# Where ScalarE empties a finished pair's bank in a slot of attention, which slots take the low parts of rows on GpSimd, and three casts of weights that change their slot

## The chip, the cores and the metric

The kernel runs on one core of a Trainium2 chip. The metric is the device time of one execution in microseconds (us). Before the change it is 763.03 us, the median of three runs (762.01 to 764.55).

## The reference, cut to what matters

For 2048 tokens of 512 features, all in fp32:

```
xn  = layernorm(x)
qkv = xn @ wqkv                       # 32 heads of 16 features each
p   = softmax(mask(q k^T / 4))        # a query sees itself and the 255 keys before it
s   = (p v) @ wo
h   = gelu(layernorm(xn) @ w1 + b1)   # 512 -> 1792
g   = silu(h @ w2 + b2)               # 1792 -> 512
out = x + s * g
```

## The kernel before, in words

**Number format.** A matrix product is made of three products of fp32r parts: a value is split into a high part (a cast) and a low part (the value less its high part), and high x high, high x low and low x high are added up. So every operand needs a cast, mostly on ScalarE, and a subtraction, on VectorE or GpSimd.

**Slots.** The attention is a hand-written schedule of 128 slots, `for t in range(-16, end + 1)` near the end of `mixer_kernel`: slot t handles group n = t // 16 of four heads and key block t % 16 of 128 keys. Every recorded instruction stands at L42, the line of the helper that keeps program order, so groups are told apart by their tiles' names. One slot issues, in this order on TensorE:

1. `prob_block(n, kb, 1)`: two matmuls of scores into the tile `stb`, which is one pair of banks for all slots; ScalarE's exponential reads it and writes `pt`; GpSimd then cuts `pt` at the band's edges (two selects).
2. `max_block` for 12 slots ahead: scores into `xy` and, where there is a block two back, into columns 0 to 255 of `zo`; VectorE merges them with a predicated copy and reduces them to row maxima (`mt`).
3. `fill_in(t, 0)`: a share of other work (below), then the entries of `plan` for slot t, which `at` puts there: casts, low parts, DMA issues.
4. `prob_block(n, kb, 0)`: the second two matmuls into `stb`, the second exponential, two more selects.
5. `fill_in(t, 1)`: more of the other work.
6. `pv_step`: 24 matmuls of the slot before into `otb`, columns 256 to 383 of the second bank of `zo`, which ScalarE copies out to `oraw`.
7. the entries of `ends`, which `behind` puts there: mostly DMA issues.

Every engine does its instructions in that order. The next slot's step 1 writes `stb` again, so it waits until the second exponential has read it.

**Tandems.** The other work of slots 3 to 127 is `tandem(t0, t1, one, two)`: two products of 512 columns made at the same time, one on rows 0 to 63 and one on rows 64 to 127 of TensorE, in the banks `fb[0]` and `fb[1]`; a unit is one matmul of each. At the end slot t1 the pair is finished: `one` is copied out of `fb[0]` by ScalarE and `two` out of `fb[1]` by VectorE (the last two lines of `tandem`). The next tandem starts in slot t1 + 1 and its first unit writes `fb[1]` and then `fb[0]`. There are 22 tandems, with end slots 8, 14, 19, 24, 30, 35, 41, 47, 53 (projections of q and k: `pair_qk`), 58, 63, 68, 74 (of v: `pair_v`), 79, 84, 90, 98 (of q and k), and 104, 110, 115, 121, 127 (hidden units of the MLP: `pair_h`). Slots 91 and 92 hold transposes of y in `fb`, and slot 128 a product of the MLP in `fb[0]`.

**What a finished pair of q and k sets off.** `pair_qk.finish(ps, t, copy)` copies the bank to `pjr`, casts it to `sh` on ScalarE in slot `free` (t + 1 for the even chunk of 512 tokens, t + 3 for the odd one, or later if the rows are still in use; for the very first pair's even chunk in the end slot itself, through `behind`), sends the high rows by four DMAs of SyncE, subtracts on GpSimd in the slot that `quiet` gives (`pjr<-pjr,sh`), and sends the low rows by two DMAs. `quiet(t)` returns the first slot from t on that is 1 or 2 modulo 4 and not yet taken. Slots that are 3 modulo 4 end with GpSimd's work on the row maxima (`max_rows`).

**Weights.** `split_wqk` casts the q and k weights of the next group on ScalarE (`wqb<-wqkr`) and subtracts on VectorE; `fetch_wqk` loads them four slots ahead. `settle` does the same for slices of w1 (tile `xnT`) and w2 (tile `w`).

**After the slots** follow the MLP's products, the output projection and the gate, in which nothing is touched.

Of the kernel before, what the change touches and what calls it, by code (L numbers as in the profile page):

```python
# [49 lines left out]
def mixer_kernel(ctx, tc, x, wqk, wv, wo, w1, b1, w2, b2, out):  # L50


    nc = SimpleNamespace(**{name: Ordered(tc, name) for name in ("tensor", "vector", "scalar", "gpsimd", "sync")})
# [141 lines left out]
    fb = [psf.tile([P, 512], F32, name=f"fb{i}") for i in range(2)]  # L195
# [92 lines left out]
    fills = {}  # L288
# [71 lines left out]
    def pair_qk(n, c):  # L360
# [11 lines left out]
        def finish(ps, t, copy):  # L372
            hi = sgp.tile([P, 512], F32R, tag="sh", name=f"sh_{n}_{c}", bufs=2)
            raw = t2.tile([P, 512], F32, tag="t2", name=f"pjr_{n}_{c}")
            lo = raw.bitcast(F32R)
            copy(raw, ps)

            def send_high():
                if n >= 2:
                    copy_rows(slots[n % 2][3:P:32, 0, :, sl], slots[n % 2][7:P:32, 0, :, sl])  # L380
                for qk, tt in ((1, 0), (0, 0), (1, 2), (0, 1)):
                    send(hi, qk, tt)

            def send_low():
                send(lo, 1, 1)
                send(lo, 0, 2)


            free = t if (n, c) == (1, 2) else max(t + 1 + 2 * (c % 2), 16 * n - 28 + 4 * c)
            free += 2 * (t == 90)  # L390
            (behind if free == t else at)(free, nc.scalar.copy, hi, raw)
            behind(free, send_high)
            free = quiet(max(free, t + 1))
            at(free, lambda: nc.gpsimd.tensor_tensor(lo, raw, hi.bitcast(F32), op=ALU.subtract))
            behind(free, send_low)
        return 3 * KT, mm, finish

    def quiet(t):

        while t % 4 not in (1, 2) or t in taken:  # L400
            t += 1
        taken.add(t)
        return t

    taken = set()
# [28 lines left out]
    def tandem(t0, t1, one, two, mid=None, back=None):  # L434

        n = one[0]
        lo, hi = slice(0, 64), slice(64, P)
        mid = mid or max(1, (t0 + t1 + 1) // 2)  # L440
        most = n // 4

        def places(slots, last):

            last = min(most, n // (len(slots) + 1)) if last else 0
            cuts = [(n - last) * k // len(slots) for k in range(len(slots) + 1)]
            out = []
            for t, a, b in zip(slots, cuts, cuts[1:]):
                ahead = min(b - a, max(most, (b - a + 1) // 2))
                out += [(t, 0)] * ahead + [(t, 1)] * (b - a - ahead)  # L450
            return out + [(t1, 0)] * last

        first, second = places(range(t0, mid), False), places(range(back or mid, t1), True)
        for phase, where in enumerate((first, second)):
            for i in range(n):
                flags = dict(start=(phase == 0 and i == 0), stop=(phase == 1 and i == n - 1), skip_group_check=True)
                def unit(i=i, phase=phase, flags=flags):
                    (two if phase == 0 else one)[1](fb[1 - phase], i, hi, **flags)
                    (one if phase == 0 else two)[1](fb[phase], i, lo, **flags)
                fills.setdefault(where[i], []).append((unit, ()))  # L460
        fills[t1, 0].append((one[2], (fb[0], t1, nc.scalar.copy)))
        fills[t1, 0].append((two[2], (fb[1], t1, nc.vector.tensor_copy)))

    def spread(jobs, places):
# [180 lines left out]
    def at(t, fn, *args):  # L645
        plan.setdefault(t, []).append((fn, args))
# [36 lines left out]
    n, raw = raws["qk"]  # L683
# [25 lines left out]
    for place, todo in spread([job_qk(1, 0), job_qk(1, 1)], [(-2, 0), (-1, 1), (-1, 1), (-1, 1), (0, 0), (0, 1)] +  # L709
                              [(t, k) for t in (1, 2) for k in range(2)]).items():  # L710
        fills.setdefault(place, []).extend(todo)
    soon = {}
    tandem(3, 8, pair_qk(1, 2), pair_qk(1, 3))
    for n, spans in enumerate((((9, 14), (15, 19)), ((20, 24), (25, 30)), ((31, 35), (36, 41)), ((42, 47), (48, 53, 51)),
                               ((75, 79), (80, 84)), ((85, 90), (93, 98))), 2):
        for c, span in zip((0, 2), spans):
            tandem(*span[:2], pair_qk(n, c), pair_qk(n, c + 1), *span[2:])
    for i, (t0, t1) in enumerate(((54, 58), (59, 63), (64, 68), (69, 74))):
        tandem(t0, t1, pair_v(2 * i), pair_v(2 * i + 1))
    for f, *span in ((6, 99, 104, 102), (8, 105, 110), (10, 111, 115), (12, 116, 121, 118, 119), (2, 122, 127, 124, 125)):  # L720
        tandem(*span[:2], pair_h(f), pair_h(f + 1), *span[2:])

    for n, t in enumerate((-5, 5, 17, 28, 38, 70, 80), 1):
        at(t - 4, fetch_wqk, n)
        at(t, split_wqk, 0)
        at(t, split_wqk, 1)
    at(20, fetch_wv, 1)
    at(23, split_wv_part, 0)
    at(26, split_wv_part, 1)
# [8 lines left out]
    on_pool = nc.gpsimd  # L738
# [4 lines left out]
                 (1, 105), (4, 105), (5, 107)):  # L743
        at(t, fetch, "w1", f)
    for f, t, lo_at, lo_by in ((6, 94, 96, nc.vector), (7, 95, 97, on_pool), (8, 96, 98, on_pool), (9, 97, 100, nc.vector),
                               (10, 100, 101, nc.vector), (11, 101, 102, nc.vector), (12, 103, 105, on_pool),
                               (13, 105, 106, on_pool), (2, 106, 108, nc.vector), (3, 107, 109, on_pool),
                               (0, 108, 110, on_pool), (1, 109, 112, nc.vector), (4, 111, 113, on_pool),
                               (5, 112, 114, on_pool)):
        at(t, settle, "w1", f, nc.scalar.copy)  # L750
        at(lo_at, settle, "w1", f, None, lo_by)
# [92 lines left out]
    for f in range(6, NF, 2):  # L844
        t = gp.tile([P, 2, 512], F32, tag="ohl", name=f"hr_{f}", bufs=4)
# [421 lines left out]
```

## Time and profile before

| what | us |
|---|---|
| median of three runs | 763.03 (762.01 to 764.55) |
| the profiled execution, its own time | 761.15 |
| span of its instructions | 759.4 |
| TensorE matmuls busy | 742.0 |
| VectorE busy | 513.2 |
| ScalarE busy | 439.9 |
| GpSimd busy | 299.7 |

The profiled execution is 1.88 us under the median, and 1.75 us of its time lie outside the span. Times in timelines are us from the span's start: slot 0 starts at 63.8, slot 41 at 184.6 and slot 127 at 431.9. In a row of a timeline stand the start, the duration, the engine (PE is TensorE's matmuls, PEld its weight loads, DVE VectorE, ACT ScalarE, POOL GpSimd, SPq SyncE's queue), the operation, output <- inputs, the sizes, the number of instructions merged into the row, and in brackets how long the engine had been idle and what ended that. A usual slot takes 2.8 us. PE's matmul ends are modelled, and consecutive matmuls overlap in the rows.

### The profile page before, as it was taken

The page shows a single profiled execution, that of the slowest core. Times are in us where ns is not written, and L with a number is a line of the kernel's source. Part 1 is how long each engine was busy: PE and PEld are TensorE (multiplying, and loading weights), DVE is VectorE, ACT ScalarE, POOL GpSimd, SP SyncE. Part 2 cuts the span into 40 slices and gives each one's busy share as a digit, 9 for nine tenths or more (in the row PEclk, how much of TensorE's full clock was granted, in tenths as well). Part 3 has the DMA queues.
Part 4 walks back from the last instruction along what each step waited for, and adds up shares of the span by engine and source line. Part 5 has one row for each costly group of instructions (what it writes and reads, how often), then busy time and mean ns, then how long its engine had stood idle before and what let it go on. Part 6 is the DMA issues. An engine that isn't in the chain of part 4 may idle for free.

```text
span 759.4 us, 18803 instructions
## 1 busy us (share of the span) xinstructions
PE 742.0 (98%) x7428; PEld 580.8 (76%) x7428; DVE 513.2 (68%) x781; ACT 439.9 (58%) x746; POOL 299.7 (39%) x644
## 2 busy tenths in 40 slices
PE   9999999999999999999999999999999999999997
PEld 8886676666778887676676688888878888888886
DVE  7886776877776677887873548763667765676373
ACT  7747767867666676777777745444554643442001
POOL 6413757767566554767867700120102000001102
PEclk9999999999999999999999999999999999999999
DMA  8623355655457753546734383542113232254531
GB/s 287 185 63 82 87 131 135 169 116 121 99 124 234 244 177 90 140 113 169 191 100 158 97 296 102 177 146 74 41 30 109 84 112 70 69 162 130 170 93 56
DMA packets 56952, 99.40 MB, mean 131 GB/s; under 512 B 11104, under 2 KB 11360, under 8 KB 56864
## 3 DMA queue, kind: packets, MB, share of 16 engines
q1 hardware_dynamic: 56864, 98.21, 44.9%
q8 instruction: 58, 0.95, 0.5%
q14 instruction: 30, 0.25, 0.1%
HBM read 51.39 MB, written 29.62 MB: 107 GB/s over the span
## 4 chain that ended last, share of the span: by engine, by line
PE 88%; ACT 5%; DVE 2%; DMA 2%; issue 2%; POOL 1%; SPq 1%; ACTq 0%; DVEq 0%; POOLq 0%
PE acc L42 20%; PE fb L42 18%; PE zo L42 12%; PE p L42 9%; PE stb L42 8%; PE h L42 6%; PE s L42 6%; PE xy L42 5%; ACT pt L42 3%; PE pv L42 3%; POOL pt L42 1%; DMA x<-in_x_dram 1%; DMA qk<-pjr 1%; PE yt L42 1%; DVE xy L42 1%
## 5 line engine op out<-in xcount | busy, mean ns | idle before, releaser
L42 POOL TENSOR_SCALAR_AFFINE_SELECT pt<-pt 128x256 f32<-128x256 f32 x480 | 194.7, 430 | 138.2 <-ACT pt L42 135.0
L42 ACT ACTIVATE pt<-stb 128x768 f32<-128x768 f32 (+1 forms) x244 | 188.7, 773 | 54.8 <-PE stb L42 44.9
L42 DVE TENSOR_REDUCE mt<-xy 128x4 f32<-128x1024 f32 (+1 forms) x128 | 152.6, 1192 | 4.4
L42 PE MATMUL acc<-w,gh 128*128 128x512 f32 x432 | 134.6, 393 | 0.0
L42 DVE COPY_PREDICATED xy<-upper,zo 128x512 f32<-128x512 int32 x112 | 77.9, 696 | 76.5 <-PE zo L42 73.1
L42 PE MATMUL fb<-xnT,wqb 64*128 64x512 f32 (+1 forms) x684 | 114.7, 404 | 0.1
L42 POOL TENSOR_TENSOR xo<-xo,gated 128x512 f32<-128x512 f32 x15 | 20.2, 1350 | 219.0 <-DVE gated L42 195.2
L42 PE MATMUL stb<-qk 64*128 64x384 f32 (+1 forms) x488 | 97.6, 396 | 7.9 <-ACT pt L42 6.4
L42 PE MATMUL zo<-pt,vt 128*17 128x128 f32 x2880 | 103.8, 275 | 0.3
L42 PEld LDWEIGHTS zo<-pt,vt 128*17 128x17 f32 x2880 | 67.4, 97 | 36.7 <-issue 19.3
L42 PEld LDWEIGHTS acc<-w,gh 128*128 128x128 f32 x432 | 80.9, 188 | 17.2
L42 PEld LDWEIGHTS stb<-qk 64*128 64x128 f32 x488 | 45.6, 183 | 55.6 <-ACT pt L42 46.4
L42 PE MATMUL acc<-w,gl 128*128 128x512 f32 x216 | 84.4, 391 | 0.0
L42 PEld LDWEIGHTS fb<-xnT,wqb 64*128 64x128 f32 (+1 forms) x684 | 63.5, 186 | 6.9 <-issue 0.6
L42 PE MATMUL xy<-qk 64*128 64x256 f32 (+2 forms) x536 | 60.2, 298 | 1.8 <-DVE mt L42 1.2
L42 ACT COPY oraw<-zo 128x128 f32<-128x128 f32 x128 | 34.2, 267 | 38.6 <-PE zo L42 33.3
L42 PEld LDWEIGHTS xy<-qk 64*128 64x128 f32 x536 | 44.4, 185 | 10.1 <-DVE mt L42 3.8
L42 PEld LDWEIGHTS acc<-w,gl 128*128 128x128 f32 x216 | 40.5, 188 | 9.3 <-DVE gl L42 0.2
L42 ACT ACTIVATE gated<-acc 128x512 f32<-128x512 f32 x16 | 8.7, 596 | 64.9 <-DVE acc L42 64.9
L42 PE MATMUL s<-wos,ohl 128*128 128x512 f32 (+1 forms) x204 | 44.8, 378 | 0.0
L42 PEld LDWEIGHTS s<-wos,ohl 128*128 128x128 f32 x204 | 36.7, 188 | 7.1
L42 ACT COPY p<-p 128x512 f32<-128x512 f32 x21 | 12.3, 585 | 50.1 <-PE p L42 42.7
(192 smaller groups left out, 1185.6 us busy)
## 6 DMA issues: line engine op xcount, KB each, us to landing
qk<-sh SPq DMA_DIRECT2D x128, 128.0 KB
qk<-pjr SPq DMA_DIRECT2D x64, 128.0 KB
oT_d<-oraw SPq DMA_DIRECT2D x32, 256.0 KB
w_d<-in_w_dram SPq DMA_DIRECT2D x14, 512.0 KB
x<-in_x_dram SPq DMA_DIRECT2D x16, 256.0 KB
or<-oT_d SPq DMA_DIRECT2D x16, 256.0 KB
w<-rden_d SPq DMA_DIRECT2D x16, 256.0 KB
xo<-in_x_dram SPq DMA_DIRECT2D x16, 256.0 KB
```

What stands on the lines that cost most here:

```text
L42: r = issue(*args, **kwargs)
```

## The change

Four edits, in one function each:

- in `tandem`, ScalarE's copy out of `fb[0]` goes from `fill_in(t1, 0)` to `fill_in(t1, 1)`: behind the second exponential of the end slot instead of ahead of it, and still ahead of the copy of `otb`. Since `finish` of `two` now runs first, it also claims its quiet slot first;
- `quiet` takes slots that are 0, 1 or 2 modulo 4;
- the q and k weights of group 3 are cast and subtracted in slot 16 instead of 17, those of group 7 cast in slot 78 instead of 80 (subtracted in 80 as before), and their loads move along by as much;
- slice 11 of w1 is cast in slot 102 instead of 101 and subtracted in 103 instead of 102.

```diff
     def quiet(t):

-        while t % 4 not in (1, 2) or t in taken:
+        while t % 4 == 3 or t in taken:
             t += 1
...
                 fills.setdefault(where[i], []).append((unit, ()))
-        fills[t1, 0].append((one[2], (fb[0], t1, nc.scalar.copy)))
+        fills.setdefault((t1, 1), []).append((one[2], (fb[0], t1, nc.scalar.copy)))
         fills[t1, 0].append((two[2], (fb[1], t1, nc.vector.tensor_copy)))
...
-    for n, t in enumerate((-5, 5, 17, 28, 38, 70, 80), 1):
+    for n, (t, low) in enumerate(((-5, -5), (5, 5), (16, 16), (28, 28), (38, 38), (70, 70), (78, 80)), 1):
         at(t - 4, fetch_wqk, n)
         at(t, split_wqk, 0)
-        at(t, split_wqk, 1)
+        at(low, split_wqk, 1)
...
-                               (10, 100, 101, nc.vector), (11, 101, 102, nc.vector), (12, 103, 105, on_pool),
+                               (10, 100, 101, nc.vector), (11, 102, 103, nc.vector), (12, 103, 105, on_pool),
```

## The prediction, made before the changed kernel was run

> **What bounds the kernel now.** I read the page first, then the table of waits, then the timeline slot by slot.
>
> ```profile
> PE 742.0 (98%) x7428; PEld 580.8 (76%) x7428; DVE 513.2 (68%) x781; ACT 439.9 (58%) x746; POOL 299.7 (39%) x644
> ...
> PEld stb L42 <- ACT pt L42: 46.4, 158, 1.0
> PE stb L42 <- ACT pt L42: 6.4, 18, 0.7
> ```
>
> TensorE's matmuls leave 759.4 - 742.0 = 17.4 us idle in the whole span. Weight loads wait 46.4 us for an exponential, but earlier matmuls mostly still run meanwhile; matmuls themselves stand still for it 18 times, 6.4 us in all. That is all that a better order on ScalarE can win from this wait. The stalls lie mainly in end slots. Slot 41 and the first half of 42 show one whole:
>
> ```profile
> 185.19 0.81 ACT L42 ACTIVATE pt<-stb 128x768 f32<-128x768 f32 x1 [0.16 <-POOL pt L42]
> ...
> 186.30 0.59 ACT L42 COPY pjr<-fb 128x512 f32<-128x512 f32 x1 [0.30 <-PE fb L42]
> ...
> 186.78 0.82 ACT L42 ACTIVATE pt<-stb 128x768 f32<-128x768 f32 x1
> ...
> 187.48 0.27 ACT L42 COPY oraw<-zo 128x128 f32<-128x128 f32 x1
> 187.49 0.68 DVE L42 COPY pjr<-fb 128x512 f32<-128x512 f32 x1
> 187.65 0.45 PE L42 MATMUL stb<-qk 64*128 64x384 f32 x2 [0.38 <-ACT pt L42]
> ...
> 188.05 0.31 PEld L42 LDWEIGHTS zo<-qk 64*128 64x128 f32 x4
> ...
> 188.22 0.82 ACT L42 ACTIVATE pt<-stb 128x768 f32<-128x768 f32 x1 [0.46 <-PE stb L42]
> 188.28 0.53 PEld L42 LDWEIGHTS fb<-xnT,wqb 64*128 64x128 f32 x6
> ...
> 189.57 0.81 ACT L42 ACTIVATE pt<-stb 128x768 f32<-128x768 f32 x1 [0.53 <-PE stb L42]
> ```
>
> The copy of fb[0] starts at 186.30 and holds the second exponential to 186.78. In the undisturbed slot 42 the two exponentials start 189.57 - 188.22 = 1.35 apart, so without the copy it would start at 185.19 + 1.35 = 186.54, 0.24 earlier. Slot 42's first scores follow its start by 187.65 - 186.78 = 0.87 and would come at 187.41. TensorE's stall there is 0.38, so 0.24 seems free.
>
> **The copy behind the exponential: what is late next.** Two things are, both in the next slot.
>
> First, VectorE's copy of the other bank. It stands behind the row maxima's reduction, which the change doesn't move, and ends at 187.49 + 0.68 = 188.17. The next tandem's first unit writes that bank. The wait costs about 0.05 after the end, as in slot 20, where it already ends last (122.59 + 0.68 = 123.27, weights at 123.32):
>
> ```profile
> 122.59 0.68 DVE L42 COPY pjr<-fb 128x512 f32<-128x512 f32 x1
> ...
> 123.32 0.53 PEld L42 LDWEIGHTS fb<-xnT,wqb 64*128 64x128 f32 x6
> ```
>
> So the unit can't start before 188.22; now it starts at 188.28.
>
> Second, the copy of `otb` (`oraw`). It now stands behind the moved copy, and the zo matmuls of the next slot wait for it: the list of compiled instructions names that wait at each of them. Its new time: an instruction follows an exponential by 187.48 - 186.78 = 0.70 and a copy of a bank by 186.78 - 186.30 = 0.48, so the moved copy starts at 186.54 + 0.70 = 187.24 and `oraw` at 187.72; it ends at 187.99, and zo's weights load at 188.04 instead of 188.05. The fb weights follow by 188.28 - 188.05 = 0.23, at 188.27. Everything that TensorE does from zo on keeps its time: the 0.24 becomes a wait for `oraw` inside slot 42. Only slot 42's first exponential comes earlier, worth at most 0.1 where ScalarE ends the second half of that slot last.
>
> [...]
>
> Of the 22 end slots I count by these bounds:
>
> - 10 (14, 19, 30, 35, 47, 63, 68, 79, 110, 115): 0. VectorE's copy or reduction ends last already in the next slot, or the exponential isn't late.
> - 7 (24, 41, 58, 74, 90, 98, 104): both bounds, between 0 and -0.1 each; I take -0.05, so -0.35.
> - slot 84: no zo matmuls follow in slot 85 and the reduction is short, so the stall of the copy goes (below).
> - 4 where the move loses: 8, 53, 121, 127.
>
> **The four losses.** In slot 8 the cast `sh` stands right behind `oraw`:
>
> ```profile
> 87.73 0.81 ACT L42 ACTIVATE pt<-stb 128x768 f32<-128x768 f32 x1 [0.16 <-POOL pt L42]
> ...
> 89.33 0.82 ACT L42 ACTIVATE pt<-stb 128x768 f32<-128x768 f32 x1
> ...
> 90.17 0.64 ACT L42 CAST sh<-pjr 128x512 fp32r<-128x512 f32 x1
> ...
> 90.73 0.81 ACT L42 ACTIVATE pt<-stb 128x768 f32<-128x768 f32 x1
> ```
>
> Slot 8's second exponential goes from 89.33 to 87.73 + 1.35 = 89.08 and `oraw` to 89.08 + 0.70 + 0.48 = 90.26; with 0.14 from there to the cast (the end of a copy of 0.27 less an overlap of 0.13) it starts at 90.40, and slot 9's exponential as far behind it as now, 90.73 - 90.17 = 0.56, at 90.96: **+0.23**. In slot 53 the copy already lies beside TensorE's work and delays nothing; behind the exponential it delays zo:
>
> ```profile
> 220.34 0.59 ACT L42 COPY pjr<-fb 128x512 f32<-128x512 f32 x1
> ...
> 220.83 0.81 ACT L42 ACTIVATE pt<-stb 128x768 f32<-128x768 f32 x1
> ...
> 222.10 0.31 PEld L42 LDWEIGHTS zo<-qk 64*128 64x128 f32 x4
> ```
>
> `oraw` ends at 220.83 + 0.70 + 0.48 + 0.27 = 222.28, zo loads at 222.33 instead of 222.10: **+0.23**. From slot 116 on there are no zo matmuls and no reductions, and the first scores use xy, so no exponential gates the next slot; but fb[0] itself comes free later:
>
> ```profile
> 419.38 0.58 ACT L42 COPY hr<-fb 128x512 f32<-128x512 f32 x1
> 419.85 0.83 ACT L42 ACTIVATE pt<-stb 128x768 f32<-128x768 f32 x1
> ...
> 420.23 0.19 PEld L42 LDWEIGHTS fb<-yh,xnT 64*128 64x128 f32 x2
> ...
> 432.96 0.59 ACT L42 COPY hr<-fb 128x512 f32<-128x512 f32 x1 [0.27 <-PE stb L42]
> 433.45 0.39 ACT L42 ACTIVATE pt<-stb 128x256 f32<-128x256 f32 x1
> 433.70 0.19 PEld L42 LDWEIGHTS fb<-yh,xnT 128*128 128x128 f32 x1 [0.21 <-ACT hr L42]
> ```
>
> Slot 121: the exponential can start at the earliest where the copy now does, at 419.38; then fb[0] is free at 419.38 + 0.70 + 0.58 + 0.05 = 420.71, against the second load of a row that starts at 420.23, about 420.32. That is 0.39 at least: **+0.4**. Slot 127, with an exponential of half the length (the copy follows by 0.39 - 0.11 = 0.28): 432.96 + 0.28 + 0.59 + 0.05 = 433.88 against 433.70, and some hundredths more until the scores are there: **+0.2**. TensorE has no idle time after either to take it up. The losses sum to 1.06.
>
> **The casts.** In slots 17 and 101 two casts hold the second exponential:
>
> ```profile
> 114.31 0.81 ACT L42 ACTIVATE pt<-stb 128x768 f32<-128x768 f32 x1
> 115.02 0.61 ACT L42 CAST wqb<-wqkr 128x512 fp32r<-128x512 f32 x1
> 115.53 0.62 ACT L42 CAST sh<-pjr 128x512 fp32r<-128x512 f32 x1
> 116.05 0.81 ACT L42 ACTIVATE pt<-stb 128x768 f32<-128x768 f32 x1
> ...
> 116.91 0.44 PE L42 MATMUL stb<-qk 64*128 64x384 f32 x2 [0.72 <-ACT pt L42]
> ...
> 362.90 0.61 ACT L42 CAST xnT<-xnT 128x512 fp32r<-128x512 f32 x1
> ...
> 363.41 0.62 ACT L42 CAST sh<-pjr 128x512 fp32r<-128x512 f32 x1
> 363.93 0.81 ACT L42 ACTIVATE pt<-stb 128x768 f32<-128x768 f32 x1
> ...
> 364.79 0.44 PE L42 MATMUL stb<-qk 64*128 64x384 f32 x2 [0.28 <-ACT pt L42]
> ```
>
> One cast of 0.61 fits into the 1.35 between two exponentials; two don't. In slot 17 the second exponential returns from 116.05 to 114.31 + 1.35 = 115.66: **-0.39**, of a stall of 0.72. In slot 101 the same, but there the matmuls stand only 0.28; between 0.28 and 0.39 I take **-0.34**. In their new slots 16 and 102 stands no other cast, and the load of group 3 is issued as far ahead as before, so I cost them at nothing; on VectorE the subtraction of 1.1 us now ends just ahead of slot 17's predicated copy, and if it doesn't, up to 0.3 of the gain is lost. The cast taken out of slot 80 delayed nothing: TensorE was held by VectorE's copy there. 0.
>
> **The low parts.** The rows are the group of GpSimd's selects and that of its low parts (count, then shortest, median and longest in ns):
>
> ```profile
> L42 POOL TENSOR_SCALAR_AFFINE_SELECT pt<-pt 128x256 f32<-128x256 f32 x480 | 194.7, 430 | 138.2 <-ACT pt L42 135.0
> ...
> L42 POOL TENSOR_TENSOR pjr<-pjr,sh x28: 1267/1281/1297, 70.4 to 367.0; 128x512 fp32r<-128x512 f32 x28
> ```
>
> Four selects of 0.43 and a low part of 1.28 make 3.0 in a slot of 2.8, so a select may start 1.3 to 1.5 late after two slots; it is needed only by the last 8 of the next slot's 24 matmuls, a slot later, so I cost it at nothing; two in a row stand in the kernel already. If a select were late, what it is late by would be paid once per low part. The earlier sending is worth something where rows come late, in slot 84:
>
> ```profile
> 312.46 0.44 PE L42 MATMUL xy<-qk 64*128 64x128 f32 x4 [0.53 <-DMA qk<-pjr]
> ```
>
> The low rows of group 6's first chunk are subtracted in slot 81 and sent behind two writes to DRAM; now in slot 80 and ahead of them, about a slot earlier. The stall of 0.53 goes. With the copy's 0.24, worked out for slot 41, which nothing holds here: **-0.77**. At no other first use of rows does a matmul stand for such a send.
>
> **The sum.** -0.35 - 0.77 - 0.39 - 0.34 + 1.06 = -0.79 us. On the profiled execution's 761.15 that is 760.4. The median of the runs is 1.88 above it, and against the median I forecast 763.03 - 0.8 = **762.2**. About 0.3% (2.3 us) is what a measurement of this kernel can tell from no change.
>
> **The rivals.**
>
> A, **the stalls do go**: zo and VectorE's copy don't hold the next slot as I take it. The stalls of 0.38 speak for it, slot 20 and the compiled wait against it. The 7 slots then give 7 x 0.24 = 1.7 instead of 0.35, and five of the ten others 1.2: -0.79 - 1.35 - 1.2 = -3.3, or 759.7.
>
> B, **`oraw` comes later than worked out**, so zo loses more than the exponential gains. My 188.04 lies only 0.01 ahead of break-even. Without the overlaps of 0.12 and 0.11, which I read from other pairs of instructions, `oraw` ends 0.23 later, in some 11 slots: +2.5, and the 0.35 is gone: -0.79 + 0.35 + 2.5 = +2.1, or 765.1.
>
> C, **the move does nothing either way**, and only the casts and slot 84's rows count: -0.39 - 0.34 - 0.53 = -1.3, or 761.8. For it speaks that my gains and losses by the move are small and each rests on a few hundredths.
>
> **How the numbers follow.** My forecast 0.50, C 0.17, A 0.24, B 0.09. Within 0.3% (760.74 to 765.32) lie the forecast, C but for 0.03, and half of B; so faster 0.27, within 0.68, slower 0.05. The range takes in A less a little and B: 759.4 to 764.9 leaves out about 2 in 10.
>
> **What would show it.** Right: in slot 42 the stall ahead of stb falls to about 0.15 and zo's weights wait for `oraw`; fb's first weights stay where they are, 188.28 - 185.19 = 3.1 behind the first exponential of slot 41. The stalls of slots 17, 101 and both of slot 84 go; slots 9, 54 and 122 grow. Wrong: that distance falls to 2.9 (A) or grows to 3.3 (B); selects appear in the chain of waits in slots 0 modulo 4; the xy stall of slot 84 is still there.

## The result and the profile after

The changed kernel takes 765.63 us, the median of 8 runs (764.46 to 766.77); the kernel before took 762.08 in 8 runs beside them (761.39 to 764.55). The ratio is 1.0043 (95% interval 1.0030 to 1.0055): the change makes the kernel 3.3 us slower by the ratio. The forecast was 762.2, and the range ended at 764.9. The profiled execution after takes 765.31 us, with a span of 763.6.

The page after, first part, TensorE's row:

```profile
PE 747.1 (98%) x7428; PEld 585.1 (77%) x7428; DVE 513.3 (67%) x781; ACT 439.4 (58%) x746; POOL 299.3 (39%) x644
```

The table of waits after (in all, times, longest):

```profile
PEld stb L42 <- ACT pt L42: 37.8, 141, 0.6
...
PE stb L42 <- DMA qk<-mT_d: 2.6, 2, 2.4
...
PE stb L42 <- ACT pt L42: 1.7, 5, 0.3
```

The change does what it says: matmuls stand still for an exponential 5 times and 1.7 us in all, where it was 18 times and 6.4. But a wait is there that the table of before does not have: the scores wait 2.4 us for `qk<-mT_d`, the read-back of the row maxima. And TensorE is busy 5.1 us longer with as many matmuls: 1.6 us of that lie in slots 69 to 71, 1.0 us ahead of slot 0, and the rest is spread over the span.

I measured each slot in both timelines from its first scores to those of the next one. Ahead of slot 0, where the code is the same, the profile after is 0.8 us later. From slot 0 to the end it loses 3.4 us more, in these places:

| place | forecast | profiles, after less before |
|---|---|---|
| slots 65, 69, 70 (no end slots) | 0 | +0.27, +2.48, +1.43 |
| the 7 ends with "both bounds" and the slots behind them | -0.35 | -0.80 |
| the 10 ends counted at nothing | 0 | -0.24, and +0.34 at 115 |
| slot 84 | -0.77 | -0.74 |
| slot 17 | -0.39 | -0.38 |
| slot 101; slots 102 and 103 | -0.34; 0 | -0.35; +0.47 |
| slots 8/9, 53/54, 121 to 124, 127 | +1.06 | +0.23, +0.14, +0.26, +0.25 |

Without the first row the others add up to -0.82, against a forecast of -0.79. So nearly all of the miss lies in slots that the prediction did not look at.

The timeline after, TensorE in slots 69 and 70; the rows of `fb` are the first units of each slot:

```profile
268.98 0.44 PE L42 MATMUL stb<-qk 64*128 64x384 f32 x2
...
272.84 0.44 PE L42 MATMUL stb<-qk 64*128 64x384 f32 x2 [2.41 <-DMA qk<-mT_d]
...
273.62 1.65 PE L42 MATMUL fb<-wva,xnT 64*128 64x256 f32 x12
...
275.00 0.58 PE L42 MATMUL stb<-qk 64*128 64x384 f32 x2
...
277.83 0.94 PE L42 MATMUL fb<-wva,xnT 64*128 64x256 f32 x12
```

The same stretch after in windows (stretch: length, busy time of each engine, granted clock of TensorE, busy share of the DMA engines, GB/s):

```profile
core 0: us, PE busy (x) PEld busy (x) DVE busy (x) ACT busy (x) POOL busy (x), PEclk, DMA share, GB/s
263.50:270.00 6.50, 6.32 (x116) 4.97 (x118) 5.10 (x8) 4.67 (x8) 3.98 (x12) 1.00 0.91 283
...
275.00:277.10 2.10, 2.10 (x35) 1.50 (x32) 1.53 (x2) 0.81 (x1) 0.64 (x3) 0.58 0.54 217
```

Two things are to be seen. The scores that open slot 70 stand 2.41 us for the read-back, behind a stretch in which the DMA engines are 91% busy. Before, the same stretch is 97% busy without such a wait, so the share alone does not decide. Then the granted clock falls, to a mean of 0.58 of full speed in the second window, and twelve matmuls take 1.65 us where in the next slot they take 0.94: slot 70 pays 1.43 us more with nothing waiting. Two of the 8 runs (764.46 and 765.11 us) have a mean granted clock of 1.000, which leaves no room for such a stretch (3.41 us at 0.5, as in the profile after, take 0.002 off the mean), and are still more than 2 us slower than the kernel before: the half clock adds to the loss, and is not the whole of it.

Why the read-back is late is seen on SyncE's queue. Before (x4 and x2 are issues merged into a row, which lasts from the start of the first to the end of the last, with the waits between them):

```profile
254.58 2.50 SPq L42 DMA_DIRECT2D qk<-sh  x4
257.17 0.56 SPq L42 DMA_DIRECT2D mT_d<-mT  x1
258.10 0.54 SPq L42 DMA_DIRECT2D oT_d<-oraw  x1
...
260.34 1.20 SPq L42 DMA_DIRECT2D qk<-pjr  x2
...
263.43 0.57 SPq L42 DMA_DIRECT2D qk<-mT_d  x1
```

After:

```profile
254.23 5.10 SPq L42 DMA_DIRECT2D qk<-sh  x4
259.43 1.28 SPq L42 DMA_DIRECT2D qk<-pjr  x2
261.45 0.56 SPq L42 DMA_DIRECT2D mT_d<-mT  x1
262.11 0.55 SPq L42 DMA_DIRECT2D oT_d<-oraw  x1
...
265.29 0.57 SPq L42 DMA_DIRECT2D qk<-mT_d  x1
```

The low rows (`qk<-pjr`) of group 5's last chunk are now subtracted in slot 64 and sent ahead of the write of the row maxima (`mT_d<-mT`), which goes from 257.17 to 261.45. Only a part of that is these two sends: the four high sends ahead of them (`qk<-sh`) take 5.10 us from first to last instead of 2.50. The second to the fourth of these are issued 0.02 after an earlier transfer on the queue has landed (256.41, 257.55 and 258.78), whose semaphore they use again.

Behind the write stands a store of `oraw` to DRAM (`oT_d<-oraw`), and the read-back lands behind that store. By the last updates of their semaphores, the store lands at 265.30 before and at 269.40 after, 7.2 and 7.3 us after its issue, and the read-back at 269.28 and 272.71, 3.98 and 3.31 us behind the store. The issue of the read-back goes from 263.43 to 265.29 only, and it is not what decides: in runs 1 and 9 (below) it is issued later still, at 267.06 and 266.29, and lands earlier. Slot 70's scores had room for 0.6 us in this execution before; they start, without a wait, at

```profile
269.91 0.44 PE L42 MATMUL stb<-qk 64*128 64x384 f32 x2
```

From issue to landing the read-back takes 5.9 us before and 7.4 after. Between the store and the read-back stand stagings of weights, DRAM to DRAM, of 512 KB each. After, every transfer issued on this queue from 242 to 268 us lands behind the one issued ahead of it; before, in the same stretch, all but one do, a copy `qk<-qk` that is issued at 253.33 and lands at 259.54, 0.11 ahead of the staging issued before it.

### The profile page after: what moved, and what is told of

Read it like the earlier page. It is cut to its first block, busy times and chain, and to the rows that moved or that the text cites. A ratio compares the mean times of both kernels' runs of the same rounds, so it can differ in the third digit from the quotient of the medians.

```text
span 763.6 us, 18800 instructions
## 1 busy us (share of the span) xinstructions
PE 747.1 (98%) x7428; PEld 585.1 (77%) x7428; DVE 513.3 (67%) x781; ACT 439.4 (58%) x746; POOL 299.3 (39%) x644
## 4 chain that ended last, share of the span: by engine, by line
PE 89%; DVE 3%; ACT 3%; DMA 2%; issue 1%; SPq 1%; DVEq 0%; ACTq 0%
PE acc L42 19%; PE fb L42 18%; PE zo L42 14%; PE p L42 9%; PE stb L42 8%; PE h L42 6%; PE s L42 6%; PE xy L42 6%; PE pv L42 3%; ACT pt L42 3%; DMA qk<-mT_d 2%; DVE xy L42 1%; DVE mt L42 1%; PE yt L42 1%; SPq L42 1%
## 5 line engine op out<-in xcount | busy, mean ns | idle before, releaser
L42 PE MATMUL zo<-qk 64*128 64x128 f32 x448 | 41.5, 262 | 0.0
```

The lines of the kernel that those rows point to most:

```text
L42: r = issue(*args, **kwargs)
```

## The experiments

Theory: the low parts' new place on SyncE's queue makes read-backs late, and the half clock adds to it. Rivals: the copy behind the exponential costs the time, or the casts' new slots do, and the wait only shows where TensorE ran ahead. All ratios are to the kernel before, timed on the same chip.

**1. The changed kernel without slot 64.**

```diff
-        while t % 4 == 3 or t in taken:
+        while t % 4 == 3 or t == 64 or t in taken:
```

> The changed kernel with one thing undone: group 5's last low part is subtracted in slot 65 again instead of 64, so its two sends stand behind the write of the row maxima (mT_d) on SyncE's queue, as before the change; all other edits stay. Theory (the loss is the late read-back of the row maxima that slot 70's scores wait for, 2.48 us of stall in slot 69 and 1.43 us of half clock behind it): both go, 3.9 us less than the changed kernel, about 0.8 below the kernel before (ratio 0.999), the matmuls of slot 70 wait for nothing and the granted clock stays at 1.00 there. Rivals (the copy behind the exponential, or the casts' new slots, cost the time and the wait at slot 70 only shows where TensorE ran ahead): stays at about 765, ratio 1.004, with the loss elsewhere.

Measured: 762.31 us, ratio 0.9999 (0.9990 to 1.0008). By the ratio, one low part put back a slot takes away the whole loss against the kernel before, and there is no half clock in the profile. But 0.8 of the forecast gain is missing, and its profile (763.63 us, the longest of the 11 runs) shows the wait, shorter, and once earlier:

```profile
260.18 0.44 PE L42 MATMUL stb<-qk 64*128 64x384 f32 x2 [1.31 <-DMA qk<-mT_d]
...
272.28 0.44 PE L42 MATMUL stb<-qk 64*128 64x384 f32 x2 [0.76 <-DMA qk<-mT_d]
```

Slots 65 and 69 lose 1.39 and 0.84 in it, 2.23 together, against 2.75 in the profile after. So the waits for read-backs are mostly still there.

**2. The low parts alone.** `quiet` as in the change; the rest as before.

> The kernel before with the low parts in three slots of four alone; copy and casts as before. Theory (late read-back at slot 70): the whole loss is here, +3.9 at slots 69 and 70, some +0.3 at slot 65, -0.5 at slot 84: about +3.7, ratio 1.005. Rival 'the copy' or 'the casts': not above the kernel before, ratio 0.999 to 1.000.

Measured: 765.95 us, ratio 1.0044 (1.0031 to 1.0056). The edit alone costs what the whole change costs, in slots 69 (+2.56), 70 and 71 (+1.06, +0.31, the half clock again), 65 (+0.74) and 101 (+1.00, the read-back of slot 102).

**3. The copy alone.** `fills.setdefault((t1, 1), [])...` as in the change; the rest as before.

> The kernel before with only ScalarE's copy of a finished pair's bank behind the slot's exponentials. Theory: the end slots as the two traces show them, about -1.3 where the exponential comes earlier and +1.1 at slots 9, 54, 122 and 127: -0.2 to -0.3, ratio 1.000; no stall at slot 70. Rival 'the copy costs it': +3 to +4, ratio 1.004 to 1.005. The prediction's own count of this edit was -0.35 - 0.24 + 1.06 = +0.5.

Measured: 765.99 us, ratio 1.0052 (1.0038 to 1.0065). The theory missed by 4 us, and by the time alone the rival would be right. The place of the loss says otherwise. The timeline of the copy alone, around slot 20:

```profile
116.21 3.37 SPq L42 DMA_DIRECT2D qk<-sh  x4
...
119.68 3.88 SPq L42 DMA_DIRECT2D qk<-pjr  x4
...
125.75 0.44 PE L42 MATMUL xy<-qk 64*128 64x128 f32 x4 [2.78 <-DMA qk<-mT_d]
```

Four low sends stand in a row, where the kernel before had two at 117.22 and two at 121.71. `finish` of the pair's second chunk now runs first and, with slots 1 and 2 modulo 4 alone, claims slot 17; the first chunk, whose rows are wanted first, gets 18, and its sends come last of the four. Slot 20's scores `xy` wait for these two: in the trace the last of them lands at 125.29, and the wait for it ends at 125.37. The releaser in brackets is inferred, and here it is not the one that holds: the read-back lands at 125.67, after the scores' wait for its semaphore has ended, at 125.48. With the new `quiet` the first chunk gets 16 and the second 17. So in the whole change, the edit that delays the read-back also repairs what the copy's move does to the order of claims: the two costs, of 3.8 us each by the medians, do not add up. Not all of run 3's loss is the order of claims: its profile loses 2.73 in slot 20 and 1.41 in slot 69, where run 4 loses 1.08 with the old order too.

**4. The casts alone.**

> The kernel before with only the three casts of weights in other slots (group 3's cast in 16, group 7's in 78, the cast of w1's part 11 in 102 with its subtraction in 103). Theory: slots 17 and 101 gain 0.38 and 0.35, slots 102 and 103 lose 0.27 and 0.20 where VectorE runs late behind the moved subtraction, so -0.3, ratio 1.000. Rival 'the casts cost it': +3 or more. The prediction's count of this edit was -0.39 - 0.34 = -0.73, ratio 0.999.

Measured: 760.98 us, ratio 0.9983 (0.9974 to 0.9992), 1.3 us faster. Slots 17 and 101 gain 0.38 and 0.35, slots 102 and 103 lose nothing, and slot 84 gains 0.74, which I had not expected (below).

**5. The copy, with the old order of claims.** ScalarE runs its instructions in the order of run 3, SyncE its transfers in that of the kernel before:

```diff
-        fills[t1, 0].append((one[2], (fb[0], t1, nc.scalar.copy)))
+        moved = lambda raw, ps: fills.setdefault((t1, 1), []).append((nc.scalar.copy, (raw, ps)))
+        fills[t1, 0].append((one[2], (fb[0], t1, moved)))
```

> The kernel before with only ScalarE's copy moved, but the finishing of the pair entered in the old order: ScalarE runs its instructions in the order of the run with the copy alone, SyncE its transfers in the order of the kernel before. Theory (the copy alone cost 3.8 us because its finish is now entered after that of the pair's other chunk, so that the low rows of three pairs are subtracted and sent in swapped order and slot 20 waits 2.78 us for rows that come last): that wait goes; what is left are the end slots, about -0.2 to -0.5, ratio 0.999 to 1.000. Rival (the copy's new place on ScalarE costs it): ratio stays near 1.005.

Measured: 762.00 us, ratio 1.0002 (0.9991 to 1.0013). The sends stand apart again and `xy` waits for nothing:

```profile
117.71 1.20 SPq L42 DMA_DIRECT2D qk<-pjr  x2
...
122.19 2.46 SPq L42 DMA_DIRECT2D qk<-pjr  x2
...
123.29 0.44 PE L42 MATMUL xy<-qk 64*128 64x128 f32 x4
```

So the copy's place on ScalarE costs nothing that can be measured; the order of its bookkeeping did.

**6 and 7. The stagings apart**, in the changed kernel and in the kernel before: those of slots 63 to 70 go to slots 71 to 78.

```diff
-        behind(55 + k, stage_in, kind, j)
+        behind(55 + k + 8 * (k > 7), stage_in, kind, j)
```

> The changed kernel with the second eight of the sixteen stagings of weights (DRAM to DRAM, one a slot in slots 55 to 70) moved from slots 63 to 70 to slots 71 to 78; SyncE's order around the low parts and the read-backs stays. Theory (read-backs of the row maxima come late because sends and stagings fill the queue ahead of them): the stalls at slots 65, 69 and 70 go, 4.2 us less than the changed kernel, about 761.4, ratio 0.999. Rival (the order of the low parts alone decides, the stagings do not matter): ratio stays above 1.003.

> The kernel before with the same eight stagings moved to slots 71 to 78. Theory: the read-back of slot 70, which landed 0.63 us ahead in the profiled run of before and late in the profile of the casts alone (1.09 us, same queue order), comes in time always: between 0 and -1, ratio 0.9985 to 1.000; and the changed kernel with stagings apart is 0 to 0.8 faster than this. Rival (the stagings play no part): ratio 1.000, and the changed kernel stays 3 us slower.

Measured: 761.10 us, ratio 0.9987 (0.9979 to 0.9996), and 762.00 us, ratio 0.9997 (0.9988 to 1.0006). With SyncE's order of low parts and read-backs as changed, the loss goes as soon as the stagings are out of the way; slot 70 of run 6 opens without a wait:

```profile
269.46 0.45 PE L42 MATMUL stb<-qk 64*128 64x384 f32 x2
...
270.20 0.93 PE L42 MATMUL fb<-wva,xnT 64*128 64x256 f32 x12
```

The read-back now lands 0.78 us behind the store of `oraw`, at 266.55. The low part ahead of the write and the stagings are both needed for the whole of the loss. With it gone, the changed kernel is 0.9 us faster than the kernel before with the same stagings, close to the prediction's sum of 0.79. The agreement is in part luck: in these two profiles the slots add up to the same time within 0.04 us, since slot 105 of run 6 loses 0.92.

**8. The changed kernel without slots 56, 60 and 64** for low parts.

> The changed kernel without low parts in slots 56, 60 and 64 (they go to 57, 61 and 65 as before), all else as changed. Theory (each low part ahead of the write of the row maxima delays the read-back two slots on): the stall of 1.39 in slot 65, which the run without slot 64 showed, goes as well and that of slot 69 shrinks to that of the kernel before: about 761.4, ratio 0.999. Rival (that stall is the stagings' own spread from execution to execution): as without slot 64 alone, 762.3, ratio 1.000.

Measured: 761.16 us, ratio 0.9984 (0.9975 to 0.9993). Slot 65 loses nothing in its profile and slot 69 0.43.

**9. The subtraction left in slot 64, the two sends one slot later.**

```diff
-            behind(free, send_low)
+            behind(free + (free == 64), send_low)
```

> The changed kernel with the last low part of group 5 still subtracted on GpSimd in slot 64, but its two transfers issued with slot 65, behind the write of the row maxima. Theory (their place on SyncE's queue delays the read-back): as the run without slot 64, about 762.3, ratio 0.999 to 1.000, no half clock behind slot 70. Rival (the subtraction itself, in front of GpSimd's selects, does it): as the changed kernel, 765.6, ratio 1.004.

Measured: 762.34 us, ratio 1.0005 (0.9993 to 1.0017), and no half clock. The subtraction in front of GpSimd's selects costs nothing here; by the ratios, the place of two transfers on SyncE's queue costs some 3 us. Its profile (762.55 us) still loses 0.83 and 1.26 in slots 65 and 69. Where the lateness comes from is seen when the times are counted from the start of slot 64 in each profile (us; landings by the semaphores):

| | before | run 8 | run 9 | changed |
|---|---|---|---|---|
| store of `oraw` issued | 5.89 | 6.88 | 8.50 | 9.80 |
| store landed | 13.09 | 14.08 | 15.77 | 17.09 |
| read-back landed | 17.07 | 18.07 | 19.75 | 20.40 |
| slot 70's scores | 17.70 | 18.21 | 19.88 | 20.53 |

In each the read-back lands 3.3 to 4.0 us behind the store. The low parts of slots 56 and 60, which run 9 has and run 8 has not, make it 1.68 us later, and that of slot 64 makes it 0.65 later again, but the half clock of 1.43 us comes with that last step alone. By the ratios to the kernel before, the shares are the other way: 2.9 us for slot 64 (1.0043 against 1.0005) and 1.6 for the other two (1.0005 against 0.9984). Each profile is one execution; where the rest of the 2.9 lies they do not show.

**10. The low parts alone, without slots 56, 60 and 64.**

> The kernel before with the low parts in three slots of four except slots 56, 60 and 64; copy and casts as before. Theory: without the read-backs' delay the new slots of the low parts are worth only the stall at slot 84, -0.74: about 761.4, ratio 0.999; where a read-back of slots 102 or 106 comes late behind the sends and the fetches of w1 up to +1. Rival (GpSimd's selects late behind the low parts): above the kernel before, ratio 1.001 or more.

Measured: 762.29 us, ratio 0.9997 (0.9988 to 1.0006). Slot 84 gains 0.73, but slot 101 loses 0.77 to the read-back of slot 102. Neither side of the expectation is told apart: the edit is worth about nothing.

**11. The parts that gain.** The casts, the copy with the old order of claims and not in the pairs that end in slots 8, 53, 79 and 121, the low parts as before, the stagings apart.

> What the runs point to: the kernel before with the three casts in their new slots, ScalarE's copy moved with the finishing entered in the old order and only in the pairs that end elsewhere than in slots 8, 53, 79 and 121, the low parts where they were, and eight stagings in slots 71 to 78. Theory: casts -1.47, copy -1.2 (end slots and the slots behind them in the run with the queue kept, without those four pairs), stagings -0.3: about 759.2, ratio 0.996, with up to +0.9 where the read-back of slot 106 comes late. Rival (the gains of a few tenths are given back elsewhere): ratio 0.9985, as the casts alone.

Measured: 760.37 us, ratio 0.9972 (0.9960 to 0.9983), 2.1 us faster than the kernel before, and the fastest of all. In its profile slot 105 loses 1.02 us:

```profile
375.09 0.45 PE L42 MATMUL stb<-qk 64*128 64x384 f32 x2 [0.96 <-DMA qk<-mT_d]
```

It is the read-back of slot 106. By then TensorE is 2.6 us ahead of the kernel before, but the read-back is issued only 1.58 us earlier (372.94 against 374.52). In the profiles of all runs slot 105 differs from before by -0.14 to +1.02; what decides how much was not tried.

## Why the prediction was wrong

**The step that failed** is the one on the low parts: "At no other first use of rows does a matmul stand for such a send." It is true of the trace of before, and it asks the wrong question. It looks at who waits for the sends that move, and not at who stands behind them on the queue that they move past. At slot 84 I even used that the sends now pass the two writes to DRAM, and counted it as a gain; that one of the writes carries the row maxima whose read-back opens a later slot, with 0.6 us to spare in slot 70, I did not price. What the runs show in its place: with the low parts of slots 56, 60 and 64 sent ahead of the writes, the write and the store of `oraw` behind it go out 4 us later, and the read-back, which lands behind the store, comes 3.3 us later from the start of slot 64. By the ratios this costs 2.9 to 3.4 us (runs 9, 1 and 2), and 4.3 to 4.5 where the stagings or the two slots ahead go as well (runs 6 and 8); in the profile after, 1.43 of it is half clock.

**The kernel before, too**, pays part of this wait in some executions: its order stands in run 4, whose profile waits 1.01 us in slot 69, where the profile of before waits for nothing. That profile, 761.15, lies 0.9 below the median of its 8 runs. I carried the difference along as a constant between profile and median. The median of the 8 runs is also 0.95 under the 763.03 of three runs that the forecast starts from, and rival B's 765.1 lies above the range's end of 764.9, though my text says that the range takes it in.

**The copy.** Its mechanism was right. Slot 41 and the first half of 42 after:

```profile
185.50 0.81 ACT L42 ACTIVATE pt<-stb 128x768 f32<-128x768 f32 x1 [0.17 <-PE stb L42]
...
186.84 0.81 ACT L42 ACTIVATE pt<-stb 128x768 f32<-128x768 f32 x1 [0.53 <-PE stb L42]
...
187.55 0.58 ACT L42 COPY pjr<-fb 128x512 f32<-128x512 f32 x1
...
188.02 0.28 ACT L42 COPY oraw<-zo 128x128 f32<-128x128 f32 x1
...
188.35 0.30 PEld L42 LDWEIGHTS zo<-qk 64*128 64x128 f32 x4
...
188.57 0.54 PEld L42 LDWEIGHTS fb<-xnT,wqb 64*128 64x128 f32 x6
```

The exponentials start 1.34 apart (forecast 1.35), `oraw` 1.18 behind the second one (1.18), and `zo` loads 0.05 after `oraw` ends. The units of the next tandem start 3.07 behind the first exponential, where 3.1 was forecast, 2.9 for rival A and 3.3 for B. Both rivals are out. The seven ends bring 0.80 instead of 0.35: five of them 0.07 to 0.13 each, slot 104 0.26 and slot 98 nothing, where I had taken 0.05 each from between 0 and 0.1. Of the losses, 8 was right to the hundredth, 53 came to 0.14 instead of 0.23, and 127 to 0.25 instead of 0.2. In slot 121 the first load of `fb` waits for the copy as forecast, slot 122 loses 0.50 instead of 0.4, but slot 124 gives 0.24 back, where I had said that TensorE has no idle time to take it up.

**The order of claims** was in my text of the change, and not in my sum. In the whole change it happened to cost nothing; run 3 shows that without the new `quiet` it makes slot 20 wait 2.78 us, and run 5 that with the old order the loss of 3.8 us goes.

**The casts** in slots 17 and 101 came out within 0.01. "The cast taken out of slot 80 delayed nothing" was wrong. On ScalarE and SyncE before:

```profile
300.60 0.61 ACT L42 CAST wqb<-wqkr 128x512 fp32r<-128x512 f32 x1
301.11 0.62 ACT L42 CAST sh<-pjr 128x512 fp32r<-128x512 f32 x1
...
301.76 2.50 SPq L42 DMA_DIRECT2D qk<-sh  x4
```

With the casts alone:

```profile
301.69 0.61 ACT L42 CAST sh<-pjr 128x512 fp32r<-128x512 f32 x1
...
302.33 2.49 SPq L42 DMA_DIRECT2D qk<-sh  x4
...
312.88 0.34 PE L42 MATMUL xy<-qk 64*128 64x128 f32 x4
```

Slot 80 starts at 299.33 before and at 300.42 in run 4, so the cast of group 6's high rows starts 0.51 earlier in the slot, and the four sends 0.52. The low sends keep their place (7.02 and 7.05 into slot 80), and yet the wait of `xy` in slot 84 is gone: the gain of 0.74 comes with the casts alone and with the low parts alone (runs 4, 2 and 10), and once where both are made. The copy alone gains 0.21 there (run 5), near the 0.24 of the forecast, but the two do not add up: without the wait for the rows the exponential is not late, and the total came out only because the wait itself was worth more than its 0.53. That the queue ahead of the low sends clears earlier is seen in the landings: counted from the start of slot 80, the store of `oraw` ahead of them lands at 11.61 before and 11.22 in run 4, and the last low send at 13.00 and 11.90. It was not tried by itself.

**Slots 102 and 103**, costed at nothing, lose 0.35 to 0.47 in the profiles of the changed kernel and of runs 1, 6, 8 and 9, which have the casts and the new low slots, and nothing in those of runs 4 and 11, which have the casts and the old ones. So neither edit does it without the other; no run has the two without the moved copy, and where they meet was not tried. The +0.34 at slot 115 stands in the profiles of the changed kernel and of run 8, and not in those of runs 1, 6 and 9, which have the same code there: it changes from execution to execution.

## What to carry to other kernels

When a step moves, list the transfers that it issues, and then everything that stands behind them on that queue up to the next wait of the bounding engine, with the time each has to spare: a send that nobody waits for can still be the one that makes a read-back late. Count to the landing and not to the issue: here the read-back was issued 1.9 us later and landed 3.4 later, behind a store that took 7.3. When a call moves whose bookkeeping hands out slots or buffers, the order of the handing out moves with it; keep that order apart from the order of the instructions, as run 5 does. And a profile in which a wait has a few tenths to spare is one execution: look for the same order in another profile before costing the wait at nothing.

## What was not expected of the hardware

Behind a wait of 2.41 us (after) and one of 2.49 (run 2) TensorE's granted clock was 0.5 for 3.41 us each, which cost 1.4 us more; behind a wait of 2.78 us in slot 20 of run 3 it stayed at full speed. After, the wait lasts from 270.43 to 272.84 and the half clock from 273.34 to 276.76. The stretches of full clock in these three traces last whole multiples of 3.413 us, the length of the half clock: 266.24, 269.65 and 757.76 us are 78, 79 and 222 of them. So do the 484.69 us of full clock behind the half clock after (142) and the 754.35 us in the profile before (221). Laid out in steps of that length from where full clock starts, the wait of the profile after falls whole into one step (269.93 to 273.34), 2.05 us of run 2's fall into one, and run 3's is cut into 1.36 and 1.42. Where a gap falls in a step would explain that the longest one was not followed by half clock, but that is my estimate from these three gaps and was not shown: no run here moves a gap within its step, and none shows how long a gap has to be.
